# Cached attention with a gated feed-forward mix: exps and row turns at the round's end, sixteen-row units in four buffers, up weights one place earlier

## The chip, the cores and the metric

The kernel runs on one core of a Trainium2 chip. The core has five engines that run side by side, each in its own program order: TensorE (PE in the profile, its weight loads PEld), VectorE (DVE), ScalarE (ACT), GpSimd (POOL) and SyncE (SP), which issues nearly all loads. Sixteen DMA engines move the data of these loads. Engines wait for each other and for loads by counting semaphores. The metric is the device time of one execution in microseconds; before the change the median of three runs is 2543.85 us (2536.63 to 2545.87).

## The reference

One token is decoded. Attention has 32 heads with 65,536 cached keys and values of 128 bf16 numbers each; beside it stands a small gated feed-forward network, and a scalar gate mixes the two.

```python
g = _sigmoid((x * gate_w).sum(-1, keepdims=True))
q = (x @ wq).reshape(B, Sq, H, Dh).transpose(0, 2, 1, 3)      # H 32, Dh 128
scores = jnp.einsum("bhqd,bhkd->bhqk", q, k_cache) * (Dh ** -0.5)
p = _softmax(scores, axis=-1)                                 # over 65536 keys
o = jnp.einsum("bhqk,bhkd->bhqd", p, v_cache)
a = o.transpose(0, 2, 1, 3).reshape(B, Sq, H * Dh) @ wo       # 4096 to 512
b = (_silu(x @ w_gate) * (x @ w_up)) @ w_down                 # 512, 1792, 512
return g * a + (1 - g) * b
```

K and V of one head are 16.8 MB each, so 1073.7 MB of the 1087.65 MB that are read are cache.

## The kernel before

**Tiling.** A head's K (and V) is loaded in two halves of 8.39 MB: 128 partitions, each with 256 rows of 128 numbers. Two halves of K share `kr`, which has room for one and a half, and two of V share `vr`, which has room for one and a quarter; so a half can be loaded only when a part of the other half has been read. `K_ORDER` and `V_ORDER` say in which order a half is read so that the shared place comes free first.

**Scores.** K lies with keys along the row. DVE transposes 32 x 32 blocks of 32-bit words (`head_k`, L357), a unit of 32 rows at a time, into one of two buffers `kt`; PE multiplies each unit in 8 matmuls of 512 columns (`scores`, L429) and adds up all of a head's scores in the PSUM tile `psS`. `ktdone` counts transposed units, `qkdone` multiplied ones; a head has 16 units (`UN`), and the counters of a head step by `STEP` = 16.

**Softmax.** After a head's last unit: the maximum per row (DVE, L332), over the partitions (POOL, L225), the exps with their row sums (ACT, L259), the sum over the partitions (POOL, L227), a transpose of the exps from `pa` to `pb` (DVE, `head_turn`, L337) and the reciprocal of the sum (DVE, `head_norm`, L342). `head_turn` waits for the exps and for all values of the head before, which still read `pb`.

**Values.** PE multiplies the exps with V, 64 matmuls per half (`values`, L456), into `psO`; `pvdone` counts quarters. ACT scales the result by the reciprocal (`row_norm`, L245), PE turns the row to a column by four small matmuls into `psT` (`turn`, L470; the profile counts eight records), ACT scales it by the gate into `oTn` (`column`, L249).

**Order.** Everything is written out by hand, with no planner. In round r of the loop PE's order is: scores of the first half of head r+1, values of the first half of head r, scores of the second half, values of the second half. The turn of an earlier head's row stands behind the first unit of the round. On DVE the exps' transpose stands behind the next head's first K transpose, and the reciprocal behind its fourth. SP issues in one queue K half 0, V half 0, K half 1, V half 1 (L185 to L191); each waits until its place is free: K for `ktdone` (three quarters of the earlier head's units, or a quarter of its own head's), V for `pvdone` (seven eighths of the earlier head's values, or three eighths of its own).

**Start and end.** Before the loop SP loads the query weights, the first two quarters of K (head 0's first half), the gate weights, then waits for a quarter of the units, then K's third quarter, the up weights, the down weights and K's last quarter (L174 to L184). The feed-forward network is computed in the middle of head 0's scores (`mlp_up`, `mlp_down`, `mlp_steps`). After the loop the columns are regrouped and multiplied with the output weights (`regroup`, `project_groups`, `project`), with the last head's values behind that. The diff and this text call a quarter of head 0's K, loaded for itself, a half load (`first_k`, 4.19 MB).

Of the kernel before, what the change touches and what calls it, by code (L numbers as in the profile page):

```python
# [28 lines left out]
def bass_gated_mix__mha_block_cached__swiglu_ffn__decode_kernel(  # L29
# [27 lines left out]
    with ExitStack() as ctx:  # L57
# [84 lines left out]
        wob = kr[:, HN * D:H * D].rearrange("p (h n) -> p h n", n=D)  # L142
        ktb = [kt[:, b, :].bitcast(BF16).rearrange("p (j k m e) -> p j k m e", j=2, k=2, e=2) for b in range(2)]
        qcol = qw[:].rearrange("p e (g k) -> p e g k", g=5)[:, :, 0:4, 31]
# [10 lines left out]
        def pv(h, n):  # L155
            return STEP * (h + 1) + 2 * n

# [3 lines left out]
        def _(sp):  # L161
# [68 lines left out]
        def _(act):  # L230
# [3 lines left out]
            qdf = qd[:].rearrange("p h e g -> p (h e g)")  # L234
            oTf = oTn[:].rearrange("p h s -> p (h s)")

            def windows(h, more=0):
                src = qdf[:, bass.ds(STEP * h + more, STEP)].rearrange("p (e g) -> p e g", e=4)
                nc.scalar.copy(qcol, src).then_inc(s_qw, STEP)  # L239

            def row_norm(h, more=0):
                act.wait_ge(s_li, STEP * (h + 1) + more)
                act.wait_ge(pvdone, pv(h, 8) + more)
                act.wait_ge(s_pt, STEP * (h + 1) + more)
                nc.scalar.mul(orow[0:4, :], psO[0:4, :], Li[0:4, :]).then_inc(s_or, STEP)  # L245

            def column(h, more=0):
                act.wait_ge(s_pt, STEP * (h + 2) + more)
                nc.scalar.mul(oTf[:, bass.ds(STEP * (h + 1) + more, 1)], psT[:, 0:1], zb[:, 0:1]).then_inc(s_oc, STEP)  # L249

            def head_exp(h, more=0):
                act.wait_ge(qkdone, STEP * (h + 1) + more)
                windows(h + 1, more)
                act.wait_ge(s_ar, STEP * (h + 1) + more)
                nc.scalar.mul(nbias[:], amx[:], -SCALE).then_inc(s_nb, STEP)  # L255
                act.wait_ge(s_nb, STEP * (h + 1) + more)
                if h >= 1:
                    act.wait_ge(s_pb, STEP * h + more)
                nc.scalar.activation(pa[:], psS[:], ACT.Exp, bias=nbias[:], scale=SCALE,  # L259
                                     accum_out=rsum[:]).then_inc(expdone, STEP)  # L260
# [16 lines left out]
            column(H - 2)  # L277
            act.wait_ge(pvdone, pv(H - 1, 6))
# [8 lines left out]
        def _(dve):  # L287
# [56 lines left out]
            def head_k(h, more=0):  # L344
                for n in range(UN):
                    i = h * UN + n
                    b, w = n // UP, K_ORDER[n // UP][n % UP]
                    if h == 0 and n % (UP // 2) == 0:
                        dve.wait_ge(landing(("k0", b, w * UROWS)), 16)
                    if h > 0 and n % UP == 0:  # L350
                        dve.wait_ge(landing(("k", b)), 16 * h + more)
                    if i >= 2:
                        dve.wait_ge(qkdone, i - 1 + more)  # L353
                    o = kt[:, i % 2, :].rearrange("p (j r t) -> p r j t", j=2, t=32)
                    src = k_rows(b, w * UROWS, (w + 1) * UROWS)
                    src = src.bitcast(U32).rearrange("p (r j t) -> p r j t", j=2, t=32)
                    nc.vector.transpose(o, src).then_inc(ktdone, 1)  # L357
# [15 lines left out]
            nc.vector.tensor_scalar(oTn[:, H, 0:1], psT[:, 0:1], Li[:], zb[:, 0:1],  # L373
                                    ALU.mult, ALU.mult).then_inc(s_otn, 1)

        @block.tensor
        def _(pe):
# [39 lines left out]
            def scores(h, b, more=0):  # L417
                for n in range(b * UP, (b + 1) * UP):
# [3 lines left out]
                    if n == 0:  # L422
                        pe.wait_ge(s_qw, STEP * (h + 1) + more)
                        if h >= 1:
                            pe.wait_ge(expdone, STEP * h + more)
                    for k in range(2):
                        at0 = 31 - (2 * (UP * b + w) + k)
                        for je in range(4):
                            done = nc.tensor.matmul(psS[:], qw[:, je, at0:at0 + 128],  # L429
                                                    ktb[i % 2][:, je // 2, k, :, je % 2],  # L430
                                                    start=(n == 0 and k == 0 and je == 0),
                                                    stop=(n == UN - 1 and k == 1 and je == 3))
                    done.then_inc(qkdone, 1)
                    if h == 0 and n == 3 * UP // 2 - 1:
                        mlp_up()
                        mlp_down()
                    if h >= 1 and n == 0:
                        turn(h - 2, more)

            def values(h, b, more=0):  # L440
# [4 lines left out]
                if h < H - 1:  # L445
                    pe.wait_ge(landing(("v", b)), 16 * (h + 1) + more)
                for n, c in enumerate(order):
                    for r in range(c * QROWS, (c + 1) * QROWS, 4):
                        if h == H - 1 and (r == 0 or r in LAST[b]):
                            pe.wait_ge(landing(("vl", b, min(e for e in LAST[b] if e > r))), 16)  # L450
                        if h == H - 1 and b == 1 and r == HALF:
                            project(H - 2)
                            turn(H - 1)
# [5 lines left out]
                        else:  # L459
                            for j in range(4):  # L460
                                done = nc.tensor.matmul(psT[:, 0:1], v_rows(h, b, r + j, r + j + 1),  # L461
                                                        pbk[:, k, rho + j:rho + j + 1],
                                                        start=False, stop=(r + j == ROWS - 1))
                    done.then_inc(pvdone, 2)

            def turn(h, more=0):
                pe.wait_ge(s_or, STEP * (h + 2) + more)
                pe.wait_ge(s_oc, STEP * (h + 2) + more)
                for i in range(4):
# [4 lines left out]
            def project(h):  # L474
                if h < H - 1:
                    pe.wait_ge(s_oc, STEP * (h + 3))
                else:
                    pe.wait_ge(s_otn, 1)
                done = nc.tensor.matmul(psY[0:1, :], oTn[:, h + 1, 0:1], wob[:, h - HN, :],  # L479
                                        start=False, stop=(h == H - 1))  # L480
# [3 lines left out]
            def regroup():  # L484
                pe.wait_ge(s_oc, STEP * ((HN - 1) + 3))
                pe.wait_ge(s_sel4, 1)
                for c in range(4):
                    for g in range(4):
                        done = nc.tensor.matmul(psQ[:, 0, HB * c:HB * c + HB], sel4[:, c, 96 - 32 * g:224 - 32 * g],
                                                oTn[:, g + 1:HN + 1:4, 0], start=(g == 0), stop=(g == 3))  # L490
                done.then_inc(s_x1, 1)
# [54 lines left out]
```

## Time and profile before

| | |
|---|---|
| median of three runs | 2543.85 us (2536.63 to 2545.87) |
| profiled execution, its own time | 2541.62 us |
| its span, first to last instruction | 2539.8 us |
| granted clock of TensorE, mean | 0.908 |
| PE busy | 2079.5 us (82%) |
| DVE busy | 1192.9 us (47%) |
| ACT busy, POOL busy | 68.9 us, 27.1 us |
| read from memory | 1087.64 MB, 428 GB/s over the span |

The profile is one execution. Busy time of an engine is the time in which its instructions ran; weight loads (PEld) overlap matmuls. A row of the timeline has the start, the length, the engine, the line and operation, the tiles, the count of merged instructions, and in brackets how long the engine had been idle and what ended that. A row of the chain has the start, the length and what it was; the chain is followed back from the last instruction, at each step to what released it. A row of the groups has the busy time and the mean of one instruction in ns behind the first bar. A row of the windows has the stretch, its length, the busy time of PE, PEld, DVE, ACT and POOL with counts, then the granted clock, the busy share of the DMA engines and GB/s. A row of the loads ends with the microseconds from issue to landing.

### The profile page before, as it was taken

Reading aid. Unit: us, or ns where it says so; the run is one execution under the profiler, and the core shown is the slowest. Engines: PE = TensorE matmul, PEld = TensorE weight load, DVE = VectorE, ACT = ScalarE, POOL = GpSimd, SP = SyncE. Lnnn points to the kernel's source line nnn. Section 1 sums busy time; section 2 is a strip of 40 time slices with the busy share of each in tenths; the row PEclk is TensorE's granted clock in tenths of the full one; section 3 lists DMA queues with packets and bytes.
Section 4 is the critical chain, followed back from the end, with each engine's and each line's share of the span. In section 5 each row is a group of like instructions: output and inputs, shape, how many; then the busy total and the mean of one; then the engine's idle time right before and its main releaser. Section 6 shows DMA issues by size and latency. Waiting matters only on the chain.

```text
span 2539.8 us, 21029 instructions
## 1 busy us (share of the span) xinstructions
PE 2079.5 (82%) x8737; PEld 809.9 (32%) x8864; DVE 1192.9 (47%) x630; ACT 68.9 (3%) x198; POOL 27.1 (1%) x80
## 2 busy tenths in 40 slices
PE   5888878877888779878788788788878977888889
PEld 2333333322333223333333333333333323333334
DVE  4454453553544535535445345355354453544541
ACT  0000000000000000000000000000000000000000
POOL 0000000000000000000000000000000000000000
PEclk9888989989988999899898899998888989889889
DMA  9999999999999999999999999999999999999999
GB/s 413 429 431 431 429 423 424 437 433 431 429 428 429 429 429 425 428 436 429 436 433 428 420 436 428 437 432 426 429 432 427 430 430 430 439 429 430 418 430 380
DMA packets 21758, 1087.77 MB, mean 428 GB/s; under 512 B 2291, under 2 KB 2806, under 8 KB 3958
## 3 DMA queue, kind: packets, MB, share of 16 engines
q1 hardware_dynamic: 21748, 1087.65, 99.6%
q8 instruction: 7, 0.11, 0.0%
q14 instruction: 1, 0.01, 0.0%
q10 hardware_dynamic: 2, 0.00, 0.0%
HBM read 1087.64 MB, written 0.00 MB: 428 GB/s over the span
## 4 chain that ended last, share of the span: by engine, by line
DMA 69%; PE 16%; DVE 12%; issue 3%; SPq 0%; DVEq 0%; ACT 0%
DMA kr<-in_A_k_cache_dram 68%; PE psS L429 13%; DVE kt L357 12%; PE psT L470 2%; DMA vr<-in_A_v_cache_dram 1%; PE psO L456 1%; SPq L166 0%; DVEq L353 0%; PE psT L461 0%; PE psY L479 0%; ACT fin L281 0%; SPq L175 0%; DVE oTn L373 0%; SPq L176 0%; DVEq L372 0%
## 5 line engine op out<-in xcount | busy, mean ns | idle before, releaser
L357 DVE STREAM_TRANSPOSE kt<-kr 128x2048 uint32<-128x2048 uint32 x512 | 1148.4, 2286 | 1202.6 <-DMA kr<-in_A_k_cache_dram 1057.2
L429 PE MATMUL psS<-kt,qw 128*128 128x512 bf16 x3969 | 1119.4, 428 | 438.5 <-DVE kt L357 428.7
L456 PE MATMUL psO<-vr,pb 128*4 128x512 bf16 x4000 | 873.8, 379 | 1.9 <-DMA vr<-in_A_v_cache_dram 1.9
L429 PEld LDWEIGHTS psS<-kt,qw 128*128 128x128 bf16 x4096 | 391.8, 104 | 1138.9 <-issue 408.3
L456 PEld LDWEIGHTS psO<-vr,pb 128*4 128x4 bf16 x4000 | 343.0, 87 | 528.8 <-issue 24.3
L239 ACT COPY qw<-qd 128x16 bf16 (+1 forms) x33 | 8.6, 259 | 1982.4 <-PE psS L429 1975.6
L470 PEld LDWEIGHTS psT<-unit,orow 4*128 4x128 f32 x264 | 50.3, 280 | 25.9 <-issue 24.7
L332 DVE TENSOR_REDUCE mxs<-psS 128x1 f32<-128x512 f32 x32 | 22.1, 692 | 68.6 <-PE psS L429 68.6
L470 PE MATMUL psT<-unit,orow 4*128 4x1 f32 x264 | 53.1, 318 | 0.8 <-ACT orow L245 0.4
L225 POOL PARTITION_ALL_REDUCE amx<-mxs x32 | 11.2, 351 | 2407.6 <-DVE mxs L332 2407.6
L245 ACT ACTIVATE orow<-psO,Li 4x512 f32<-4x512 f32 x31 | 21.0, 677 | 354.7 <-PE psO L456 354.7
L337 DVE STREAM_TRANSPOSE pb<-pa 128x512 bf16<-128x512 bf16 x32 | 21.5, 671 | 13.2 <-PE psO L456 13.2
L259 ACT ACTIVATE pa<-psS,nbias 128x512 bf16<-128x512 f32 x32 | 22.0, 687 | 5.2 <-ACT nbias L255 5.1
L373 DVE TENSOR_SCALAR oTn<-psT,Li,zb 128x1 bf16<-128x1 f32 x1 | 0.3, 280 | 33.7 <-PE psT L461 33.7
L456 PE MATMUL psO<-kr,pb 128*4 128x512 bf16 x64 | 14.0, 379 | 0.0
L227 POOL PARTITION_ALL_REDUCE Lt<-rsum x32 | 12.3, 384 | 44.9 <-ACT pa L259 44.9
L382 PE MATMUL psM<-ones,xrow 1*128 1x1 bf16 x4 | 0.3, 172 | 13.6 <-DMA gwrow<-in_gate_w_dram 13.6
L456 PEld LDWEIGHTS psO<-kr,pb 128*4 128x4 bf16 x64 | 5.6, 87 | 8.2
L249 ACT ACTIVATE oTn<-psT,zb 128x1 f32 (+1 forms) x32 | 8.1, 254 | 1.1 <-PE psT L470 1.1
L255 ACT ACTIVATE nbias<-amx 128x1 f32<-128x1 f32 x32 | 6.5, 203 | 33.3 <-POOL amx L225 33.3
L405 PEld LDWEIGHTS psM<-xTb,vr 128*128 128x128 bf16 x112 | 6.9, 158 | 0.2
L405 PE MATMUL psM<-xTb,vr 128*128 128x1 bf16 x112 | 6.8, 198 | 0.0
(53 smaller groups left out, 56.3 us busy)
## 6 DMA issues: line engine op xcount, KB each, us to landing
kr<-in_A_k_cache_dram SPq DMA_DIRECT2D x4, 4096.0 KB, 26.5
vr<-in_A_v_cache_dram SPq DMA_DIRECT2D x3, 2048.0 KB, 23.8
vr<-in_A_wq_dram SPq DMA_DIRECT2D x1, 4096.0 KB, 12.5
kr<-in_A_v_cache_dram SPq DMA_DIRECT2D x1, 4096.0 KB, 20.5
kr<-in_A_v_cache_dram SPq DMA_DIRECT2D x2, 2048.0 KB, 26.9
kr<-in_A_wo_dram SPq DMA_DIRECT2D x1, 3584.0 KB, 31.6
vr<-in_B_w_gate_dram SPq DMA_DIRECT2D x1, 1792.0 KB, 34.9
vr<-in_B_w_up_dram SPq DMA_DIRECT2D x1, 1792.0 KB, 18.2
```

The lines of the kernel that those rows point to most:

```text
L225: nc.gpsimd.partition_all_reduce(amx[:], mxs[:], P, RMAX).then_inc(s_ar, STEP)
L227: nc.gpsimd.partition_all_reduce(Lt[:], rsum[:], P, RADD).then_inc(s_L, STEP)
L239: nc.scalar.copy(qcol, src).then_inc(s_qw, STEP)
L245: nc.scalar.mul(orow[0:4, :], psO[0:4, :], Li[0:4, :]).then_inc(s_or, STEP)
L259: nc.scalar.activation(pa[:], psS[:], ACT.Exp, bias=nbias[:], scale=SCALE, accum_out=rsum[:]).then_inc(expdone, STEP)
L332: nc.vector.reduce_max(mxs[:], psS[:], AX_X).then_inc(s_mx, STEP)
L337: nc.vector.transpose(pb[:], pa[:]).then_inc(s_pb, STEP)
L357: nc.vector.transpose(o, src).then_inc(ktdone, 1)
L405: done = nc.tensor.matmul(psM[:, o + j:o + j + 1], w[:, c, :, j], xTb[:, c:c + 1], start=(c == 0), stop=(c == Dc - 1))
L429: done = nc.tensor.matmul(psS[:], qw[:, je, at0:at0 + 128], ktb[i % 2][:, je // 2, k, :, je % 2], start=(n == 0 and k == 0 and je == 0), s ...
L456: done = nc.tensor.matmul(psO[0:4, :], pbk[:, k, rho:rho + 4], v_rows(h, b, r, r + 4), start=(b == 0 and n == 0 and r == c * QROWS), stop= ...
L470: done = nc.tensor.matmul(psT[:, 0:1], orow[0:4, i * Dh:(i + 1) * Dh], unit[0:4, i:i + 1], start=(i == 0), stop=(i == 3 and h < H - 1))
```

## The change

- A unit is 16 rows instead of 32 (`UROWS`), and `kt` has four buffers (`NKT`) of half the size; a unit takes 4 score matmuls instead of 8. `STEP` becomes 32, and `pvdone` counts 4 per quarter.
- On DVE, the exps' transpose and the reciprocal of a head stand right behind its maximum, at the end of the round, ahead of the next head's K transposes.
- On PE, the turn of the row stands at the end of the round, behind the values, instead of behind the next round's first unit, and turns the head just finished. On ACT, the row's scaling and then the column follow the exps in the same round; the loop counts heads by 1. The last heads' `turn` and `project` outside the loop move accordingly.
- `oTn` holds one column a head without gaps.
- Both halves of K count on one landing semaphore, and both halves of V on one.
- At the start, the up weights are issued ahead of SP's wait and of K's third half load.

```diff
-UROWS = 32
+UROWS = 16
...
-STEP = 16
+STEP = 32
+NKT = 4
...
-        kt = sb("kt", [P, 2, UNIT // 2], U32)
+        kt = sb("kt", [P, NKT, UNIT // 2], U32)
...
-        oTn = sb("oTn", [P, H + 1, STEP], BF16)
+        oTn = sb("oTn", [P, H], BF16)
...
         def pv(h, n):
-            return STEP * (h + 1) + 2 * n
+            return STEP * (h + 1) + 4 * n
...
             load(("wg",), w_at["wg"], w_dram["wg"])
+            load(("wu",), w_at["wu"], w_dram["wu"])
             sp.wait_ge(ktdone, UP // 2)
             first_k(1, 0, HALF)
-            load(("wu",), w_at["wu"], w_dram["wu"])
             load(("wd",), w_at["wd"], w_dram["wd"])
...
-                    load(("k", b), k_rows(b, 0, ROWS), cache_rows(k_dram, 1, b, 0, ROWS, q0))
+                    load(("k",), k_rows(b, 0, ROWS), cache_rows(k_dram, 1, b, 0, ROWS, q0))
...
-                    load(("v", b), v_rows(0, b, 0, ROWS), cache_rows(v_dram, 0, b, 0, ROWS, q0))
+                    load(("v",), v_rows(0, b, 0, ROWS), cache_rows(v_dram, 0, b, 0, ROWS, q0))
...
-            with act.Fori(0, STEP * (H - 2) + 1, STEP) as more:
-                head_exp(1, more)
-                column(-1, more)
-                row_norm(0, more)
+            with act.Fori(0, H - 1, 1) as r:
+                head_exp(1, r)
+                row_norm(0, r)
+                column(0, r)
...
-                        dve.wait_ge(landing(("k", b)), 16 * h + more)
-                    if i >= 2:
-                        dve.wait_ge(qkdone, i - 1 + more)
-                    o = kt[:, i % 2, :].rearrange("p (j r t) -> p r j t", j=2, t=32)
+                        dve.wait_ge(landing(("k",)), STEP * (h - 1) + 16 * (b + 1) + more)
+                    if i >= NKT:
+                        dve.wait_ge(qkdone, i - NKT + 1 + more)
+                    o = kt[:, i % NKT, :].rearrange("p (j r t) -> p r j t", j=2, t=32)
...
-                    if n == 0 and h >= 1:
-                        head_turn(h - 1, more)
-                    if n == 3 and h >= 1:
-                        head_norm(h - 1, more)
                 head_max(h, more)
+                head_turn(h, more)
+                head_norm(h, more)
...
-            head_turn(H - 1)
-            head_norm(H - 1)
...
-                    for k in range(2):
-                        at0 = 31 - (2 * (UP * b + w) + k)
-                        for je in range(4):
-                            done = nc.tensor.matmul(psS[:], qw[:, je, at0:at0 + 128],
-                                                    ktb[i % 2][:, je // 2, k, :, je % 2],
-                                                    start=(n == 0 and k == 0 and je == 0),
-                                                    stop=(n == UN - 1 and k == 1 and je == 3))
+                    at0 = 31 - (UP * b + w)
+                    for je in range(4):
+                        done = nc.tensor.matmul(psS[:], qw[:, je, at0:at0 + 128], ktb[i % NKT][:, je // 2, :, je % 2],
+                                                start=(n == 0 and je == 0), stop=(n == UN - 1 and je == 3))
                     done.then_inc(qkdone, 1)
...
-                    if h >= 1 and n == 0:
-                        turn(h - 2, more)
...
                         if h == H - 1 and b == 1 and r == HALF:
-                            project(H - 2)
                             turn(H - 1)
...
-                    done.then_inc(pvdone, 2)
+                    done.then_inc(pvdone, 4)
...
                 for b in range(2):
                     scores(1, b, more)
                     values(0, b, more)
+                turn(0, more)
             regroup()
-            turn(H - 2)
             project_groups()
-            for h in range(HN, H - 2):
+            for h in range(HN, H - 1):
                 project(h)
```

More of the change, by code (lines that the diff above doesn't have):

```diff
@@ L142, in bass_gated_mix__mha_block_cached__swiglu_ffn__decode_kernel @@
         wob = kr[:, HN * D:H * D].rearrange("p (h n) -> p h n", n=D)
-        ktb = [kt[:, b, :].bitcast(BF16).rearrange("p (j k m e) -> p j k m e", j=2, k=2, e=2) for b in range(2)]
+        ktb = [kt[:, b, :].bitcast(BF16).rearrange("p (j m e) -> p j m e", j=2, e=2) for b in range(NKT)]
         qcol = qw[:].rearrange("p e (g k) -> p e g k", g=5)[:, :, 0:4, 31]
@@ L234, in _, with windows, row_norm, column @@
             qdf = qd[:].rearrange("p h e g -> p (h e g)")
-            oTf = oTn[:].rearrange("p h s -> p (h s)")
-            def windows(h, more=0):
-                src = qdf[:, bass.ds(STEP * h + more, STEP)].rearrange("p (e g) -> p e g", e=4)
+            def windows(h, r=0):
+                src = qdf[:, bass.ds(16 * h + 16 * r, 16)].rearrange("p (e g) -> p e g", e=4)
                 nc.scalar.copy(qcol, src).then_inc(s_qw, STEP)
[L241 to L244, printed above, removed]
+            def row_norm(h, r=0):
+                act.wait_ge(s_li, STEP * (h + 1) + STEP * r)
+                act.wait_ge(pvdone, pv(h, 8) + STEP * r)
                 nc.scalar.mul(orow[0:4, :], psO[0:4, :], Li[0:4, :]).then_inc(s_or, STEP)
[L247 to L254, printed above, removed]
+            def column(h, r=0):
+                act.wait_ge(s_pt, STEP * (h + 1) + STEP * r)
+                nc.scalar.mul(oTn[:, bass.ds(h + r, 1)], psT[:, 0:1], zb[:, 0:1]).then_inc(s_oc, STEP)
+            def head_exp(h, r=0):
+                act.wait_ge(qkdone, STEP * (h + 1) + STEP * r)
+                windows(h + 1, r)
+                act.wait_ge(s_ar, STEP * (h + 1) + STEP * r)
                 nc.scalar.mul(nbias[:], amx[:], -SCALE).then_inc(s_nb, STEP)
-                act.wait_ge(s_nb, STEP * (h + 1) + more)
+                act.wait_ge(s_nb, STEP * (h + 1) + STEP * r)
                 if h >= 1:
-                    act.wait_ge(s_pb, STEP * h + more)
+                    act.wait_ge(s_pb, STEP * h + STEP * r)
                 nc.scalar.activation(pa[:], psS[:], ACT.Exp, bias=nbias[:], scale=SCALE,
@@ L368, in _ @@
                 head_k(1, more)
-            head_turn(H - 1)
-            head_norm(H - 1)
             dve.wait_ge(s_li, STEP * H)
             dve.wait_ge(pvdone, pv(H - 1, 8))
-            nc.vector.tensor_scalar(oTn[:, H, 0:1], psT[:, 0:1], Li[:], zb[:, 0:1],
+            nc.vector.tensor_scalar(oTn[:, H - 1:H], psT[:, 0:1], Li[:], zb[:, 0:1],
                                     ALU.mult, ALU.mult).then_inc(s_otn, 1)
@@ L445, in values @@
                 if h < H - 1:
-                    pe.wait_ge(landing(("v", b)), 16 * (h + 1) + more)
+                    pe.wait_ge(landing(("v",)), STEP * h + 16 * (b + 1) + more)
                 for n, c in enumerate(order):
@@ L475, in project @@
                 if h < H - 1:
-                    pe.wait_ge(s_oc, STEP * (h + 3))
+                    pe.wait_ge(s_oc, STEP * (h + 2))
                 else:
                     pe.wait_ge(s_otn, 1)
-                done = nc.tensor.matmul(psY[0:1, :], oTn[:, h + 1, 0:1], wob[:, h - HN, :],
+                done = nc.tensor.matmul(psY[0:1, :], oTn[:, h:h + 1], wob[:, h - HN, :],
                                         start=False, stop=(h == H - 1))
@@ L489, in regroup @@
                         done = nc.tensor.matmul(psQ[:, 0, HB * c:HB * c + HB], sel4[:, c, 96 - 32 * g:224 - 32 * g],
-                                                oTn[:, g + 1:HN + 1:4, 0], start=(g == 0), stop=(g == 3))
+                                                oTn[:, g:HN:4], start=(g == 0), stop=(g == 3))
                 done.then_inc(s_x1, 1)
```

5 lines of the change are left out of this document (2 added, 3 removed).

## The prediction

> **What bounds the kernel now.** I read the page from the totals down: the load queue first, then the chain that ended last, then one round of the loop in order of time, because a share over the whole span does not say which wait ends last in a round.
>
> ```profile
> span 2539.8 us, 21029 instructions
> PE 2079.5 (82%) x8737; PEld 809.9 (32%) x8864; DVE 1192.9 (47%) x630; ACT 68.9 (3%) x198; POOL 27.1 (1%) x80
> ...
> DMA  9999999999999999999999999999999999999999
> GB/s 413 429 431 431 429 423 424 437 433 431 429 428 429 429 429 425 428 436 429 436 433 428 420 436 428 437 432 426 429 432 427 430 430 430 439 429 430 418 430 380
> ...
> q1 hardware_dynamic: 21748, 1087.65, 99.6%
> ...
> DMA 69%; PE 16%; DVE 12%; issue 3%; SPq 0%; DVEq 0%; ACT 0%
> ```
>
> One queue moves 1087.65 MB, and its packets fill 99.6% of sixteen engines' span. The rate is flat: every slice but the first (413) and the last (380) lies between 418 and 439 GB/s. PE at 82% and DVE at 47% are below that. The chain's line seems to say otherwise, for 31% of it lies on engines. But the chain goes back from a K load to what let it be issued (a transpose on DVE, behind scores on PE), and does not ask whether the engines that move data still had an earlier load to work on. They had. One round shows it, with the column of what ended each idle time at the end of the row:
>
> ```profile
> 1017.30 0.33 SPq L166 DMA_DIRECT2D vr<-in_A_v_cache_dram  x1
> 1020.76 0.68 ACT L245 ACTIVATE orow<-psO,Li 4x512 f32<-4x512 f32 x1 [11.38 <-PE psO L456]
> 1024.70 2.31 DVE L357 STREAM_TRANSPOSE kt<-kr 128x2048 uint32<-128x2048 uint32 x1 [17.23 <-DMA kr<-in_A_k_cache_dram]
> ...
> 1027.24 3.59 PE L429 MATMUL psS<-kt,qw 128*128 128x512 bf16 x8 [6.66 <-DVE kt L357]
> ...
> 1030.76 1.78 PEld L470 LDWEIGHTS psT<-unit,orow 4*128 4x128 f32 x8 [0.84 <-issue]
> 1030.76 1.86 PE L470 MATMUL psT<-unit,orow 4*128 4x1 f32 x8
> ...
> 1038.43 0.12 DVE L342 RECIPROCAL Li<-Lt 128x1 f32<-128x1 f32 x1
> 1038.47 8.87 DVE L357 STREAM_TRANSPOSE kt<-kr 128x2048 uint32<-128x2048 uint32 x4
> ...
> 1038.67 0.33 SPq L166 DMA_DIRECT2D kr<-in_A_k_cache_dram  x1
> ...
> 1047.39 1.98 PE L429 MATMUL psS<-kt,qw 128*128 128x512 bf16 x7 [0.22 <-DVE kt L357]
> ...
> 1049.30 13.98 PE L456 MATMUL psO<-vr,pb 128*4 128x512 bf16 x64
> 1060.01 0.33 SPq L166 DMA_DIRECT2D vr<-in_A_v_cache_dram  x1
> 1063.61 4.50 DVE L357 STREAM_TRANSPOSE kt<-kr 128x2048 uint32<-128x2048 uint32 x2 [16.28 <-DMA kr<-in_A_k_cache_dram]
> ...
> 1073.90 0.33 SPq L166 DMA_DIRECT2D kr<-in_A_k_cache_dram  x1
> ...
> 1084.46 5.78 PE L456 MATMUL psO<-vr,pb 128*4 128x512 bf16 x26
> 1084.64 0.69 DVE L332 TENSOR_REDUCE mxs<-psS 128x1 f32<-128x512 f32 x1 [2.14 <-PE psS L429]
> ...
> 1086.31 0.69 ACT L259 ACTIVATE pa<-psS,nbias 128x512 bf16<-128x512 f32 x1 [0.17 <-ACT nbias L255]
> ```
>
> A load of the loop is 128 x 65,536 bytes = 8.39 MB, so at 430 GB/s it takes 19.5 us. The chain of waits has two K loads from issue to landing, and the start of the next one's transposes:
>
> ```profile
> 1038.67 24.82 DMA kr<-in_A_k_cache_dram
> 1073.90 28.26 DMA kr<-in_A_k_cache_dram
> 1102.28 2.32 DVE kt L357
> ```
>
> Each took 5.3 and 8.8 us longer than its bytes need: it stood behind the V load ahead of it. For V the same sum goes by the K landings: K lands at 1024.6 and 1063.5, so the V load issued at 1017.30 was 7.3 us early, and the one at 1060.01, the tightest of the four, 3.5 us early. How much of that is a load's own latency is bounded by the first load of the program, which stood behind nothing:
>
> ```profile
> vr<-in_A_wq_dram SPq DMA_DIRECT2D x1, 4096.0 KB, 12.5
> ```
>
> 4.19 MB need 9.8 us, so at most 2.7 us are latency. Margins before the queue runs dry are therefore 4.6 (V half 0), 2.6 (K half 1), 0.8 (V half 1) and 6.1 us (K half 0): small, but all positive. The queue is the bound, in every round, and a part of the change is worth something only if it alters the bytes, their rate, or one of these margins past zero.
>
> **The change part by part.** No byte is added or removed, and V's places and thresholds in rows stay (V half 0 after 7/8 of the earlier values, half 1 after 3/8).
>
> *Sixteen rows in four buffers.* 512 transposes of 2048 words become 1024 of 1024, and 8 score matmuls for 32 rows become 4 for 16, so PE issues as many. The price of a small transpose is not in the trace; these rows bound it:
>
> ```profile
> L357 DVE STREAM_TRANSPOSE kt<-kr 128x2048 uint32<-128x2048 uint32 x512 | 1148.4, 2286 | 1202.6 <-DMA kr<-in_A_k_cache_dram 1057.2
> L337 DVE STREAM_TRANSPOSE pb<-pa 128x512 bf16<-128x512 bf16 x32 | 21.5, 671 | 13.2 <-PE psO L456 13.2
> ```
>
> Four in a row took 8.87 us, 2.22 each, so 1.11 is the lower end. A line through 671 ns at 512 elements and 2286 at 2048 is 133 ns + 1.051 ns per element, so 1.21 is the upper; I take 1.21, the dearer, since a fixed part shows in the small one. Per half of K: 16 x 1.21 = 19.4 us against 8 x 2.22 = 17.8, at most 1.6 us more for DVE. Against it stands the head and tail: PE's first matmul came 2.54 us after DVE's start (1024.70 to 1027.24) and would come after 1.44, and the last unit on PE is 0.99 us instead of 1.98, together 2.1 us. In the second half this nets to 0.5 us sooner (1.11 would give 2.1). Of the first half most was PE's slow clock: 8 matmuls in 3.59 us against 7 or 8 in 1.98. With four slots DVE works on while PE is slow. If PE stays slow to 1036 as before, it does 5.5 of 16 units until then (1.80 us each from 1026.1) and 10.5 more at 0.99, so values begin at 1046.5 instead of 1049.30. Both halves' later issues thus move forward, none back.
>
> *The turn after PV instead of behind the first unit.* The 8 records of the turn (1.86 us) and the 0.84 us ahead of them leave the first half and go between the end of PV and the landing of K: from about 1098.4 (1084.46 + 13.98) to 1101.4 with 0.68 us of the row norm ahead, and K lands at 1102.2. It is hidden there by the wait for the load; with that cover gone it costs 2.7 us of PE per round, which is what it costs today.
>
> *The exp's transpose and the reciprocal at the round's end.* DVE now stands at the transpose of the exps until the earlier head's values are done, about 14 us, and the next head's K transposes are queued behind it in order. PE waits for those transposes, SP for the eighth of them. Exp itself is ready early (from the max at 1084.64 to the end of exp at 1087.0), so the end of PV decides: 1098.4, then 0.67 for the transpose and 0.68 + 0.12 for row norm and reciprocal, free by 1099.9. K lands 2.3 us later. Cost 0 in the path; if the cover were gone, K half 1's issue would move by the excess, and it has more room than before, for its eighth transpose ends at about 1034.5 instead of 1038.67 (unit 4 leaves PE at 1026.1 + 4 x 1.80, then 1.21). New margins by these times: about 6.8 for K half 1 and 3.6 for V half 1.
>
> *One landing semaphore for both K halves, one for both V halves; the rows of normed heads without gaps; ACT's counters from a loop by 1.* A half is issued only after the other has been read in part, so no wait passes early; the ALU work is on ACT (3% busy). Cost 0.
>
> *Up weights ahead of K's third half.* The rows of the start:
>
> ```profile
> 0.73 0.39 SPq L166 DMA_DIRECT2D vr<-in_A_wq_dram  x1
> ...
> 34.16 0.33 SPq L166 DMA_DIRECT2D kr<-in_A_k_cache_dram  x1
> 34.54 0.43 SPq L166 DMA_DIRECT2D vr<-in_B_w_up_dram  x1
> ...
> 48.46 4.51 DVE L357 STREAM_TRANSPOSE kt<-kr 128x2048 uint32<-128x2048 uint32 x2 [5.48 <-DMA kr<-in_A_k_cache_dram]
> ```
> ```profile
> 59.79 26.29 DMA kr<-in_A_k_cache_dram
> ```
> ```profile
> 30.00:50.00 20.00, 13.21 (x54) 4.54 (x52) 14.52 (x7) 0.00 (x0) 0.00 (x0) 0.99 0.98 414
> 86.20:2467.00 2380.80, 1963.52 (x7934) 756.46 (x8056) 1131.50 (x581) 62.14 (x180) 22.18 (x61) 0.91 1.00 430
> ```
>
> By 34.16, wq, two halves of K and the gate weights were queued, 14.4 MB or 33.6 us of work behind an issue at 0.73: with the latency above, dry between 34.3 and 37.0, so this issue came at the last moment or just in time. What ran dry is at most (430 - 414) / 430 x 20 us = 0.7 us. Moving 1.84 MB ahead of the wait gives 4.3 us of cover, so the gain is 0 to 0.7; I take 0.7. The price: K's third half lands 4.3 us later, at 52.7, and with four slots its last transpose ends about 9 us on, so the first K load of head 1 is issued at about 62 instead of 59.79. It landed at 86.1, so its data began to move at about 66.6; less 2.7 us the limit is 63.9. It fits by about 2 us; 1 us is the upper end of the loss. The first exps then turn at about 88 instead of behind the first unit, 2 us of DVE that the margin of 6 for the next issue covers.
>
> *The end.* The last V load's landing sets it:
>
> ```profile
> 2504.19 31.81 DMA vr<-in_A_v_cache_dram
> ```
> ```profile
> 2531.08 0.08 PEld L479 LDWEIGHTS psY<-kr,oTn 128*1 128x1 bf16 x1 [0.46 <-DMA vr<-in_A_v_cache_dram]
> 2531.08 0.38 PE L479 MATMUL psY<-kr,oTn 128*1 128x512 bf16 x1
> ```
>
> One 0.38 us projection leaves this stretch, and PE waits for a load there anyway: 0.
>
> **Sum.** The profiled execution took 2541.62 us (span 2539.8), 2.2 below the median 2543.85 of the runs shown. 2541.6 - 0.7 = 2540.9, so 2541; the loss of 1 at the start and some gaps in the tightest rounds (0.4% of the span, 10 us, is all that the queue is not busy, start and end in it) bound it to 2532 and 2543 by the profile, and the runs shown scatter over 9 us besides.
>
> **A rule against the rows.** The rate is what the sum hangs on. Observed: 430 GB/s over 2381 us, no slice above 439. The Trainium skill, DMA: Bandwidth & Descriptors, section Specifications, gives two limits: 435 GB/s for the ports into SBUF, and about 358 GB/s of HBM per core. By the second this kernel would need 3038 us, and the trace contradicts it with 428 over the span. By the first an estimate is 1087.65 MB / 435 = 2500 us and some 6 to 9 us of start and end, so 2508; the trace stays about 1% below it. Neither is used in the sum.
>
> **The rivals.**
>
> *The wait at the round's end holds up K (slower).* Place: DVE between the max and the next head's first transpose. For it: the transpose of the exps waits for all of the earlier head's values, and DVE's 17.23 us idle ahead of 1024.70 is where it goes. Against: PV ended 3.8 us before K landed, and the K behind it has some 7 us of margin. It decides once PV ends more than about 2.3 + 6.8 = 9 us later than I reckon; from there every us is paid 31 times, and 0.41 us over is already 0.5%. At 2 us over: 2541 + 62 = 2603. The small transpose is the other way to the same place: if it cost as much as a large one, a half of K would take 16 x 2.27 = 36.3 us, and with 14 us of PV behind the second half DVE would need some 89 us a round against 78; 2541 + 31 x 11 = 2880. The 671 ns of the transpose of 512 speaks against it.
>
> *The queue gets a better rate (faster).* If the margins' growth closes gaps that now stretch the packets, the rate could reach the highest slice. At 437 GB/s over the loop: 2381 x 7 / 437 = 38 us, so 2503. For it: slices of 436 to 439 exist, and V half 1 has only 0.8 us. Against: slices differ by where packets are counted, and the share is 1.00 in the loop already.
>
> **How the numbers follow.** 0.5% (12.7 us) is about what a measurement of this kernel can tell from no change. The forecast, the queue still full, within 2531 to 2556: 0.80. DVE or the round's end holding K back: 0.12, all slower. A better rate: 0.08, all faster. The range 2530 to 2558 holds the first and the near edge of each other.
>
> **What would show it right or wrong.** Right: the queue's share again above 99%, 430 GB/s in the loop, K landings 78 us a head apart, the transpose at 1.1 to 1.2 us, SP's issues earlier relative to the landing before them, the turn in the gap ahead of K. Wrong: GB/s in the loop below 425 with issues that land 22 us later (no queue ahead of them), DVE waiting for PE's values when K has landed, or a transpose above 1.4 us.

## The result and the profile after

The changed kernel takes 2522.65 us in the median of six runs (2521.34 to 2523.26); the kernel before 2543.27 in six (2536.63 to 2545.87). The ratio is 0.9924, 95% interval [0.991, 0.9938]: 20 us or 0.8% faster, where 2541 and "no change" were forecast. Beside the median the spread shrank, from 9 us to 2. The profiled execution took 2521.34 us.

From the page of the kernel after: the span, the share of the queue and the rate in 40 slices, the chain by engine, and the groups of the small transposes and of the exps' transposes at the round's end.

```profile
span 2519.5 us, 22671 instructions
...
GB/s 416 434 434 434 433 433 434 434 434 433 433 434 434 434 434 433 434 434 433 434 433 433 434 433 433 435 435 434 433 433 433 434 435 433 433 433 433 434 433 381
...
q1 hardware_dynamic: 21748, 1087.65, 99.9%
...
DMA 74%; DVE 15%; issue 6%; PE 4%; DVEq 0%; SPq 0%; ACT 0%; POOL 0%; ACTq 0%; POOLq 0%
...
L355 DVE STREAM_TRANSPOSE kt<-kr 128x1024 uint32<-128x1024 uint32 x1024 | 1162.3, 1207 | 780.2 <-DMA kr<-in_A_k_cache_dram 778.3
...
L335 DVE STREAM_TRANSPOSE pb<-pa 128x512 bf16<-128x512 bf16 x32 | 22.8, 711 | 415.5 <-PE psO L444 413.2
```

The bytes are the same. The queue's share rose from 99.6% to 99.9%, the rate in the slices from 418 to 439 GB/s to 433 to 435. The slices of before looked flat only while there was nothing to hold them against: beside these they scatter, and their mean is lower. DVE now idles 413.2 us behind the values, as the change makes it, and that costs nothing.

One round of the kernel after, in order of time, K landing at 1014.6, at 1053.3 and again 38.7 us later:

```profile
1009.45 0.68 ACT L244 ACTIVATE orow<-psO,Li 4x512 f32<-4x512 f32 x1 [11.55 <-PE psO L444]
1009.47 0.71 DVE L335 STREAM_TRANSPOSE pb<-pa 128x512 bf16<-128x512 bf16 x1 [13.33 <-PE psO L444]
...
1010.18 1.05 PE L458 MATMUL psT<-unit,orow 4*128 4x1 f32 x8 [0.85 <-ACT orow L244]
1010.26 0.16 DVE L340 RECIPROCAL Li<-Lt 128x1 f32<-128x1 f32 x1
...
1014.77 18.14 DVE L355 STREAM_TRANSPOSE kt<-kr 128x1024 uint32<-128x1024 uint32 x16 [4.35 <-DMA kr<-in_A_k_cache_dram]
1016.24 17.81 PE L422 MATMUL psS<-kt,qw 128*128 128x512 bf16 x64 [5.01 <-DVE kt L355]
1024.07 0.33 SPq L167 DMA_DIRECT2D kr<-in_A_k_cache_dram  x1
...
1034.06 13.98 PE L444 MATMUL psO<-vr,pb 128*4 128x512 bf16 x64
1044.76 0.33 SPq L167 DMA_DIRECT2D vr<-in_A_v_cache_dram  x1
1053.47 18.14 DVE L355 STREAM_TRANSPOSE kt<-kr 128x1024 uint32<-128x1024 uint32 x16 [20.56 <-DMA kr<-in_A_k_cache_dram]
```

DVE's sixteen transposes run without a stop, 1.13 us apart. The turn and the exps' transpose stand in the gap ahead of K's landing. The issue of V's second half is what moved most: 1044.76, 8.7 us ahead of the transposes of the K half that it stands behind, where the round shown of before has 3.6 (1060.01 to 1063.61).

**Where the time had been.** The trace of before holds the answer when all its rounds are sorted by that lead (from SP's issue of V's second half to DVE's first transpose of the K half ahead of it in the queue) beside the time from this K half to the next. In 9 of the 30 rounds that can be seen the lead was 5.55 to 6.39 us, and the next K half came 38.70 to 38.82 later. In the other 21 it was 2.63 to 3.88 us, and the next K half came 38.67 to 40.69 later, 39.5 in the mean. The sum over the 30 rounds above 38.7 is 17.8 us, and 2.0 in the 29 other half rounds: together 19.8 of the 20.3 us by which the spans differ. Two rounds that lost and one that did not, from the chain of waits of before (issue, and time to landing):

```profile
100.16 24.64 DMA kr<-in_A_k_cache_dram
...
135.20 29.74 DMA kr<-in_A_k_cache_dram
...
489.12 27.41 DMA kr<-in_A_k_cache_dram
...
527.71 27.52 DMA kr<-in_A_k_cache_dram
...
804.11 24.60 DMA kr<-in_A_k_cache_dram
...
837.89 31.44 DMA kr<-in_A_k_cache_dram
```

The issues of V's second half that fall between them, from the queue's order of time of before:

```profile
121.48 0.33 SPq L166 DMA_DIRECT2D vr<-in_A_v_cache_dram  x1
...
510.44 0.33 SPq L166 DMA_DIRECT2D vr<-in_A_v_cache_dram  x1
...
826.19 0.33 SPq L166 DMA_DIRECT2D vr<-in_A_v_cache_dram  x1
```

Landings are 124.80 and 164.94 (40.1 apart, V issued 3.3 before the first), 516.53 and 555.23 (38.7, V issued 6.1 before), 828.71 and 869.33 (40.6, V issued 2.5 before). The one round that the prediction shows, 1063.49 to 1102.16, is among the rounds that lost nothing.

The gap itself can be seen. These are the first, the third, the sixth, the tenth and the last of 30 stretches of before, 2 to 4 us behind the issue of V's second half; the last two columns are the busy share of the DMA engines and GB/s:

```profile
123.48:125.48 2.00, 1.27 (x6) 0.35 (x4) 0.57 (x1) 0.00 (x0) 0.00 (x0) 1.00 0.72 262
...
280.56:282.56 2.00, 1.27 (x6) 0.35 (x4) 0.48 (x1) 0.00 (x0) 0.00 (x0) 1.00 0.23 98
...
512.44:514.44 2.00, 1.28 (x6) 0.35 (x4) 0.00 (x0) 0.00 (x0) 0.00 (x0) 1.00 0.68 295
...
828.19:830.19 2.00, 1.28 (x6) 0.35 (x4) 1.37 (x1) 0.00 (x0) 0.00 (x0) 1.00 0.09 33
...
2386.76:2388.76 2.00, 1.28 (x6) 0.35 (x4) 0.34 (x1) 0.00 (x0) 0.00 (x0) 1.00 0.27 98
```

A single stretch says little, for a packet is counted whole where it starts, and one lasts 2.4 us (512.44 is of a round that lost nothing). The mean of the 30 is 0.61; that of the same 30 stretches of the kernel after is 0.96. (1 - 0.61) x 2 us is 0.8 us a round, a rough size. The packets in the trace say what the loss is made of. In the 9 us behind the issue, in the mean of the 21 rounds with a short lead and for each of the sixteen engines, 0.25 us are without a packet, and the packets last 0.52 us more in all than at 2.42 us each. Together that is 0.77 us, beside 0.84 in the intervals of these rounds. So an engine stands empty for only a third of it; the rest is slower packets behind the late issue.

### The profile page after: what moved, and what is told of

Its sections match the earlier page's. It is cut to its first block, busy times and chain, and to the rows that moved or that the text cites. A ratio compares the mean times of both kernels' runs of the same rounds, so it can differ in the third digit from the quotient of the medians.

```text
span 2519.5 us, 22671 instructions
## 1 busy us (share of the span) xinstructions
PE 2076.6 (82%) x8856; PEld 788.6 (31%) x8856; DVE 1217.7 (48%) x1142; ACT 72.2 (3%) x197; POOL 27.6 (1%) x80
## 3 DMA queue, kind: packets, MB, share of 16 engines
q1 hardware_dynamic: 21748, 1087.65, 99.9%
## 4 chain that ended last, share of the span: by engine, by line
DMA 74%; DVE 15%; issue 6%; PE 4%; DVEq 0%; SPq 0%; ACT 0%; POOL 0%; ACTq 0%; POOLq 0%
DMA kr<-in_A_k_cache_dram 72%; DVE kt L355 15%; PE psS L422 3%; DMA vr<-in_A_v_cache_dram 1%; PE psO L444 1%; DVEq L351 0%; SPq L167 0%; PE psM L399 0%; PE psY L407 0%; DVE mxs L330 0%; PE psY L467 0%; PE psT L449 0%; ACT fin L279 0%; POOL amx L226 0%; SPq L176 0%
## 5 line engine op out<-in xcount | busy, mean ns | idle before, releaser
L355 DVE STREAM_TRANSPOSE kt<-kr 128x1024 uint32<-128x1024 uint32 x1024 | 1162.3, 1207 | 780.2 <-DMA kr<-in_A_k_cache_dram 778.3
L335 DVE STREAM_TRANSPOSE pb<-pa 128x512 bf16<-128x512 bf16 x32 | 22.8, 711 | 415.5 <-PE psO L444 413.2
L458 PE MATMUL psT<-unit,orow 4*128 4x1 f32 x256 | 33.5, 248 | 27.1 <-ACT orow L244 26.4
L458 PEld LDWEIGHTS psT<-unit,orow 4*128 4x128 f32 x256 | 30.8, 186 | 43.2 <-ACT orow L244 42.0
L330 DVE TENSOR_REDUCE mxs<-psS 128x1 f32<-128x512 f32 x32 | 22.1, 692 | 40.1 <-PE psS L422 40.1
L248 ACT ACTIVATE oTn<-psT,zb 128x1 f32 x31 | 8.2, 263 | 38.0 <-PE psT L458 38.0
```

Of the source, the lines that this page charges most:

```text
L330: nc.vector.reduce_max(mxs[:], psS[:], AX_X).then_inc(s_mx, STEP)
L335: nc.vector.transpose(pb[:], pa[:]).then_inc(s_pb, STEP)
L458: done = nc.tensor.matmul(psT[:, 0:1], orow[0:4, i * Dh:(i + 1) * Dh], unit[0:4, i:i + 1], start=(i == 0), stop=(i == 3 and h < H - 1))
```

## The experiments

Four theories were set against each other. Q: the queue runs dry for some of the sixteen DMA engines because V's second half is issued too late. U: the small units themselves make the stream faster. T: the place of the turns does. S: the start does. Each first run does one part alone, or undoes one. The kernel before took 2543.5 us beside these four.

**V's second half in two pieces, nothing else.**

```diff
+                    if b == 1:
+                        sp.wait_ge(pvdone, pv(0, 1) + more)
+                        load(("va", 1), v_rows(0, b, 0, QROWS), cache_rows(v_dram, 0, b, 0, QROWS, q0))
                     sp.wait_ge(pvdone, (pv(-1, 7), pv(0, 3))[b] + more)
-                    load(("v", b), v_rows(0, b, 0, ROWS), cache_rows(v_dram, 0, b, 0, ROWS, q0))
+                    if b == 0:
+                        load(("v", 0), v_rows(0, b, 0, ROWS), cache_rows(v_dram, 0, b, 0, ROWS, q0))
+                    else:
+                        load(("v", 1), v_rows(0, b, QROWS, ROWS), cache_rows(v_dram, 0, b, QROWS, ROWS, q0))
...
+                    if b == 1:
+                        pe.wait_ge(landing(("va", 1)), 16 * (h + 1) + more)
                     pe.wait_ge(landing(("v", b)), 16 * (h + 1) + more)
```

> The kernel before with V's second half issued in two pieces: its first 64 rows (2.1 MB) as soon as the first quarter of the earlier half's values is done, the other 192 rows where the whole load stood. Nothing else moves. Theory Q (the queue runs dry for some of the DMA engines each round, because V's second half is issued too late: in the trace of before the 2 to 4 us behind that issue have a mean busy share of 0.62, so about 0.76 us is lost in each of 31 rounds, 23 us): the early piece covers 4.9 us, so 2520 to 2528 us and a share of about 1 behind that issue. Theory U (16-row units make the stream faster): 2543, no change. Theory T (the place of the turns does): 2543. Theory S (the start does): 2543.

Measured: 2526.53 us, ratio 0.9931 [0.991, 0.9953]. Of the change's parts this kernel has none, and it has 17 of the 20 us. Its page has the queue at

```profile
q1 hardware_dynamic: 26212, 1087.65, 99.9%
```

So U, T and S are not needed for the gain. They could still be a second way to it, which the next runs test.

**The units alone.** The turns, the exps' transpose, the reciprocal and the up weights go back; the shared landing semaphores and ACT's counters stay as the change has them:

```diff
+                    if n == 1 and h >= 1:
+                        head_turn(h - 1, more)
+                    if n == 7 and h >= 1:
+                        head_norm(h - 1, more)
                 head_max(h, more)
-                head_turn(h, more)
-                head_norm(h, more)
...
+                    if h >= 1 and n == 1:
+                        turn(h - 2, more)
...
-                turn(0, more)
```

> The changed kernel with the turns, the exps' transpose, the reciprocal and the up weights put back where they were before (transpose behind the second 16-row unit, reciprocal behind the eighth, turn behind the second): units of 16 rows in four buffers are what is left, with the shared landing semaphores and the counters. Theory Q: it counts by how much V's second half is issued sooner; DVE works on while PE is slow, so some 2 us sooner (5.5 us ahead of K's landing instead of 3.5): most of the gain, 2522 to 2530. Theory U: all of it, 2521 to 2525. Theories T and S: 2543.

Measured: 2521.90 us, ratio 0.9915 [0.9887, 0.9944]. All of the gain. Its leads are 5.47 to 8.17 us, and every K half comes 38.7 us behind the one before.

**The turns alone**, on the kernel before with 32-row units:

```diff
-                    if n == 0 and h >= 1:
-                        head_turn(h - 1, more)
-                    if n == 3 and h >= 1:
-                        head_norm(h - 1, more)
                 head_max(h, more)
+                head_turn(h, more)
+                head_norm(h, more)
...
-                    if h >= 1 and n == 0:
-                        turn(h - 2, more)
...
+                turn(0, more)
```

> The kernel before with only the turn on PE and the exps' transpose and reciprocal on DVE moved to the round's end; 32-row units in two buffers, up weights late. Theory Q: the first half of a round loses the turn's 2.7 us on PE, so V's second half goes out some 2 to 3 us sooner: most of the gain, 2522 to 2530. Theory U: 2543. Theory T: 2521 to 2525. Theory S: 2543.

Measured: 2524.56 us, ratio 0.9925 [0.9897, 0.9954]. Leads 5.80 to 6.97 us, and again 38.7 us from K half to K half. Three edits that do different things each bring 17 to 22 us, and the changed kernel, which has the second and the third in it, brings 20 and not their sum. That is what Q expects of three ways to issue one load sooner, and what U and T each expect of only one of them.

**The up weights back.**

```diff
-            load(("wu",), w_at["wu"], w_dram["wu"])
             sp.wait_ge(ktdone, UP // 2)
             first_k(1, 0, HALF)
+            load(("wu",), w_at["wu"], w_dram["wu"])
```

> The changed kernel with the up weights again behind SP's wait and K's third half load. Theory Q, U and T: 2522 to 2524, at most 1 us more than the changed kernel. Theory S (the start is what gained): 2543.

Measured: 2522.20 us (2521.77 to 2522.75), the changed kernel's own time. S falls; this part is worth nothing that can be measured.

**The way back: the lead made short again.** The second four start from the changed kernel and only delay the issue of V's second half: by a longer wait, and then by matmuls whose result nobody reads, ahead of the count that SP waits for. Two theories differ on the amount. M is the prediction's margin: only a lead below a load's latency of 2.7 us costs. N says that the lead means nothing. The kernel before took 2538.6 us beside these.

```diff
-                    sp.wait_ge(pvdone, (pv(-1, 7), pv(0, 3))[b] + more)
+                    sp.wait_ge(pvdone, (pv(-1, 7), pv(0, 4))[b] + more)
```

> The changed kernel with V's second half issued a quarter of the values later (after all four quarters of the earlier half's values instead of three), 3.5 us, so 5.2 us ahead of K's landing instead of 8.7. In the trace of before, rounds with that lead at 5.5 us or more have 38.7 us from this K landing to the next, rounds at 3.9 or less have 38.7 to 40.7. Theory Q (some DMA engines run dry when the lead is below a bound that lies between 3.9 and 5.5): 2521 to 2530, near the edge. Theory M (the prediction's margin: only a lead below 2.7 us costs): 2522. Theory N (the lead means nothing, the units or turns themselves do): 2522.

Measured: 2523.60 us, ratio 0.994 [0.9924, 0.9957].

```diff
+                    if h < H - 1 and b == 0 and n == 3:
+                        for _ in range(8):
+                            done = nc.tensor.matmul(psM[:], sel[:, 0, :], sel[:].rearrange("p a m -> p (a m)"), start=True, stop=True)
                     done.then_inc(pvdone, 4)
```

> As the run before, and 8 matmuls of 512 columns that nobody reads ahead of the count that lets V's second half go, 1.7 us: lead about 3.5 us, as in the kernel before. Theory Q: the loss is back, 0.5 to 1 us in each of 31 rounds, 2537 to 2553. Theory M: 2522. Theory N: 2522.

Measured: 2557.37 us, ratio 1.0075 [1.0058, 1.0092]. This is above the 2537 to 2553 that Q gave. The gain is gone and more: each of its rounds has the short lead that 21 of the 30 rounds of before had.

The same with `range(16)`:

> The same with 16 such matmuls, 3.5 us: lead about 1.7 us. Theory Q: 2 to 3 us lost in each of 31 rounds, 2580 to 2620. Theory M: 1 us a round, 2553. Theory N: 2522.

Measured: 2558.70 us, ratio 1.0075 [1.0058, 1.0092]. Half the lead, but no more lost; Q's 2580 to 2620 was wrong, and M's 2553 near. The pages of the two have the queue at

```profile
q1 hardware_dynamic: 21748, 1087.65, 99.4%
```
```profile
q1 hardware_dynamic: 21748, 1087.65, 99.2%
```

The control has the 16 matmuls behind the count:

```diff
                     done.then_inc(pvdone, 4)
+                    if h < H - 1 and b == 0 and n == 3:
+                        for _ in range(16):
+                            nc.tensor.matmul(psM[:], sel[:, 0, :], sel[:].rearrange("p a m -> p (a m)"), start=True, stop=True)
```

> Control: the changed kernel with the same 16 matmuls behind the count and V's issue where the change has it, so PE does the extra work but the lead stays at 8.7 us. Theories Q, M and N: 2521 to 2524; if the extra matmuls themselves slow the stream, as much as the run before.

Measured: 2522.06 us. The extra work costs nothing; the lead does. N falls, and M falls at 3.5 us, where it gave 2522 and 2557 was measured.

**How much lead is enough, and why.** With 3.5 us the intervals scatter from 38.67 to 40.8; with 1.7 nearly all are 39.4 to 39.8. Two more theories, for a bound above 2.7: P, an engine needs its next packet one packet's time early; J, the engines drift apart, whatever the packets. The first two runs split the K loads of the kernel with 8 matmuls in two and in four, for packets of 32 and 16 KB instead of 64; the edit shown is the first one's. The kernel before took 2538.3 us beside these four.

```diff
-                    load(("k",), k_rows(b, 0, ROWS), cache_rows(k_dram, 1, b, 0, ROWS, q0))
+                    for r0 in range(0, ROWS, ROWS // 2):
+                        load(("k",), k_rows(b, r0, r0 + ROWS // 2), cache_rows(k_dram, 1, b, r0, r0 + ROWS // 2, q0))
...
-                        dve.wait_ge(landing(("k",)), STEP * (h - 1) + 16 * (b + 1) + more)
+                        dve.wait_ge(landing(("k",)), 2 * STEP * (h - 1) + 16 * 2 * (b + 1) + more * 2)
```

> The kernel with 8 extra matmuls and the late issue (lead 3.5 us, 2557 us) and each half of K in two loads of 128 rows, so the packets of the load ahead of V's second half are 32 KB instead of 64 KB and take half of 2.4 us. Bytes, lead and all waits stay. Theory P (a DMA engine must have its next packet one packet's time early, so the bound of the lead is 2.7 us plus one packet's time: 5.1 with 64 KB, 3.9 with 32 KB): most of the loss goes, 2523 to 2537. Theory J (engines drift apart whatever the packets, and the drift sets the bound): 2550 to 2560.

Measured: 2555.99 us, ratio 1.007 [1.0046, 1.0093].

> The same with each half of K in four loads of 64 rows, packets of 16 KB. Theory P: bound 3.3 us, below the lead of 3.5: 2521 to 2527. Theory J: 2550 to 2560.

Measured: 2552.93 us, ratio 1.0057 [1.0039, 1.0075]. The packets ahead are a quarter as large, and the time is within 5 us of the 2557.37 with 64 KB. P falls. Its page has the queue at

```profile
q1 hardware_dynamic: 48532, 1087.66, 99.9%
```

So a share of 99.9% can stand beside a time 30 us above the changed kernel's: the share counts a slower packet as busy.

Two more leads, by `range(4)` and `range(12)`:

> The late issue with 4 extra matmuls instead of 8: lead about 4.35 us, between the runs with 5.27 (2523.6) and 3.5 (2557.4). Theory P (bound 5.1): a part of a packet's time lost in some engines, 2530 to 2550. Theory J: in the same range. A bound at 2.7 us: 2522.

Measured: 2532.50 us (2524.14 to 2540.70 in ten runs), ratio 0.9974 [0.9955, 0.9992], in the range that both theories gave.

> The late issue with 12 extra matmuls: lead about 2.6 us, between 3.5 (2557.4, scattered intervals) and 1.7 (2558.7, a steady loss of 0.95 us a round). Theory P: engines still differ by a packet, 2552 to 2575. If all engines wait together from 2.7 us down: about 0.1 us a round, 2525.

Measured: 2555.34 us, ratio 1.0073 [1.0047, 1.0099]. That is in P's range here; the 2525 of a bound at 2.7 us for all engines together was far off.

Put together, by the median lead of the profiled execution; the loss is what the time from this K half to the next has above 38.7 us, in the mean of its rounds:

| kernel | lead, us | loss a round, us | median, us |
|---|---|---|---|
| changed | 8.72 | 0.01 | 2522.65 |
| longer wait | 5.27 | 0.04 | 2523.60 |
| and 4 matmuls | 4.30 | 0.31 | 2532.50 |
| before | 3.70 (2.63 to 6.39) | 0.59 | 2543.27 |
| and 8 matmuls | 3.45 | 0.94 | 2557.37 |
| and 12 matmuls | 2.7 (1.74 to 3.13) | 0.85 | 2555.34 |
| and 16 matmuls | 1.70 | 1.12 | 2558.70 |

The medians were not all taken side by side: beside the kernel before at 2543.27 stands the changed one alone, and the runs of the other rows stand beside 2538.6 and 2538.3 us of the kernel before.

A lead of 5.2 us is enough. At 4.3 us 18 of 30 rounds still lose nothing and others up to 1.4; at 3.5 most lose, up to 2.1. At 1.7 nearly all lose 0.7 to 1.1, and 2.7 less 1.7 is 1.0: there the latency reckoned in the prediction fits.

The profile's views give the sixteen engines only as a sum, but the traces hold more. The landing semaphore of each load rises by 16 in sixteen single steps, at sixteen times, and what the kernel takes as the landing is the last step. The trace names no engine for a step; in the kernel after sixteen packets are under way at any time behind these issues, so a step is read here as one engine's end. In the 30 rounds of before, the K half ahead of V's second half has 1.36 to 3.10 us from its first step to its last; with 16 matmuls the middle value is 0.61. When the lead is counted to the first step and not to the landing, all kernels but the one with V in two pieces fall into two groups, 390 rounds in all:

| V's second half issued ahead of the first step by | rounds | loss a round, us |
|---|---|---|
| 2.49 us or more | 203 | 0.12 at most |
| 2.30 us or less | 187 | 0.87 in the mean; 166 lose more than 0.06 |

So the bound is between 2.3 and 2.5 us before the first engine is done, inside the latency of at most 2.7, and the rest of the lead of about 5 us is the time between the first engine's end and the last one's. That is J, and it also fits the runs with smaller packets, where the first and the last step lie as far apart (2.26 and 1.75 us in the middle, 2.34 with 64 KB). With 16 matmuls the engines end nearly together, and so a lead of 1.70 us costs little more than one of 3.45. Why the engines drift apart, and why the other 21 of the 187 rounds lose next to nothing, is not shown.

## Why the prediction was wrong

*The queue is the bound.* Right, and it stayed so: no byte changed, and the gain is in how fast the queue moved them.

*"Margins ... small, but all positive."* This is the step that failed. The lead of 3.5 us for V's second half was right, and so was the latency of at most 2.7; but the rest of 0.8 us was taken for safety, as if the sixteen engines were one that finishes at once. In the round that the prediction reads, the first of the sixteen steps came at 1061.61 and the last at 1063.50, with the issue at 1060.01: to the first it was 1.6 us and not 3.5, so the margin was 1.1 us below zero. The runs show a loss that begins between 5.2 and 4.3 us of lead and is 0.6 to 0.9 us a round around 3.5. The margins were also worked out from one round, and by luck that round is one of three among the 21 with a short lead that lost nothing.

*"The share is 1.00 in the loop already."* A figure with two places can hide what is at stake: 0.5% of 2381 us is 12 us, and 433 instead of 430 GB/s is 0.7%. The page's 99.6% left 10 us, and the time fell by 20: the share does not count all that a late load costs, for the slower packets behind it are counted as busy.

*The rival "a better rate".* Its mechanism is what happened, the right margin was named with it (V's second half), and it got 8 in 100. Its price of 2503 went by the highest slice, and was too much; the sum of the intervals above 38.7 would have given some 2522. The ceiling of 435 GB/s that the Trainium skill gives (DMA: Bandwidth & Descriptors, Specifications) is not passed: the slices of the kernel after lie at 433 to 435.

*The small transposes.* Right: 1207 ns in the mean against 1.21 us taken, 1.13 us apart in a row, where the bounds were 1.11 and 1.21.

*The turn and the exps' transpose hidden ahead of K.* Right in place: DVE is free at 1010.4, 4.35 us before it goes on, where 2.3 was forecast. The rival in which this wait holds K up did not happen.

*The first half sooner by 2.8 us.* Too little: values begin 19.3 us behind DVE's start (1014.77 to 1034.06) instead of 24.6 (1024.70 to 1049.30). The forecast let PE's slow clock last to 1036, as before. Windows of before and of the kernel after, with the granted clock third from the end:

```profile
1026.00:1028.00 2.00, 0.76 (x2) 0.28 (x3) 2.00 (x3) 0.00 (x0) 0.00 (x0) 0.50 1.06 459
1028.00:1036.00 8.00, 7.78 (x23) 3.69 (x23) 4.11 (x2) 0.00 (x0) 0.00 (x0) 0.50 0.98 426
```
```profile
1016.00:1018.00 2.00, 1.76 (x5) 0.64 (x6) 2.00 (x3) 0.00 (x0) 0.00 (x0) 0.50 1.06 459
1018.00:1020.00 2.00, 2.00 (x6) 0.65 (x5) 2.00 (x3) 0.00 (x0) 0.00 (x0) 0.50 1.06 459
1020.00:1022.00 2.00, 2.00 (x10) 0.84 (x9) 2.00 (x3) 0.00 (x0) 0.00 (x0) 0.93 0.91 393
```

Nearly nine microseconds at half clock behind PE's first matmul (1027.24 to 1036) became about four (1016.24 to 1020.3). In the mean of the first halves of 30 rounds the traces have 7.1 us before and 4.3 after, 6.4 in the run with the units alone, which keeps the turn between them, and 4.4 in the run with the turns alone. So most of it came with moving the turn and the exps' transpose together, which the forecast left out; the two were not tried apart. This made the lead 8.7 instead of the 6.3 that the forecast implies, and either is enough.

*The up weights.* 0 to 0.7 us of gain were allowed and 0.7 taken; the run with them put back shows none.

## What to carry to other kernels

A load queue that is 99.6% busy is not yet full: sort all rounds by how far ahead each load is issued, and put the time to the next landing beside it. What counts is the lead to the first engine's end, which in the kernel before lay up to 3.1 us ahead of the landing. Where the short leads have the long intervals, any edit that issues that load sooner is worth the same sum once, and the cheapest of them will do. Do not take a margin of one round, or a share with two places, for proof that nothing is lost.

## What was not expected of the hardware

A load of 8.39 MB had to be issued about 5 us before the landing of the load ahead of it, though the latency seen on an idle queue is at most 2.7 us, and packets of a quarter the size did not change that. Counted to the first of the sixteen steps of that landing, 2.5 us were enough in all rounds. Below this the loss hardly grows with the delay: 0.94 us a round at a lead of 3.45 us, 1.12 at 1.70, where the sixteen end nearly together.
